# Attention as one table of fine steps, batched routing, and spaced place writes in a three-stage Trainium2 kernel

## The chip, the cores and the metric

One core of one Trainium2 chip runs the whole program. The metric is device time in microseconds for one execution. Engine names: PE is TensorE (matmuls and transposes), DVE is VectorE, ACT is ScalarE, POOL is GpSimd, SP is the engine that issues most DMAs.

## What is computed

Three layers in a row on float32 data, with B=2, H=8, S=768, D=48 and N=1536 tokens of width 384:

```python
# 1. gated linear attention, per head: a decaying, turning complex state
scale = min(|a|, 0.999) / (|a| + 1e-6);  a = (a_re + i a_im) * scale
S = a[t] * S + k[t] v[t]^T               # D x D per head, S complex
y[t] = q[t] @ Re(S)
# 2. a mixture of 8 experts, one per token, capacity 2N/E
e = argmax(x @ w_gate);  gate = softmax(x @ w_gate)[e]
out = gate * (relu(x @ w1[e]) @ w2[e])   # dropped beyond the capacity
# 3. RMS norm and a gated feed-forward layer
xn = x / sqrt(mean(x*x) + 1e-6) * rms_g
out = (silu(xn @ w_gate) * (xn @ w_val)) @ w_out
```

## The kernel before

**Order.** Every compute engine and SP is wrapped in `InOrder`, which chains the instructions of an engine in the order in which the program emits them. So the order of work on each engine is written by hand, and an engine whose next instruction waits holds back all that stands behind it.

**Attention** goes over 12 chunks of 128 tokens (six per sequence), with the gates of two chunks at a time in a group. For a group `squares`, `logs_1` to `logs_4` turn the gates into log decays and tangents (ACT with the table of Ln and Exp, DVE, and POOL for the sum of squares and one product), `sums` and `decays` make the running decay (PE, ACT) and send its last row to DRAM (`ends`), from which `ends_in` fetches it in another layout (`re`). `angles_1` to `angles_4` and `turns` make the running angle (ACT with the table of Arctan and Sin, PE, DVE). For a chunk `scaled` and `frame` form the turned keys and queries (DVE, `kqr`, `K`, `Q`), `flip` transposes them (PE, copied out by ACT as `KT`, `QT`), `scores` multiplies them (PE, tile `ap`) and masks them (DVE, `AT`), `end_decay` transposes `re` (PE, `rp`), `state_up` and `state` update the state (PE `up`, DVE `z`, POOL `st`), `outputs` forms the output (PE `yp`, copied out as `yT`) and `route_1` turns it back to token order and makes the routing logits (PE `xb`, DVE `lg_all`).

**Routing.** `choice` finds a token's expert by five small DVE instructions, `route_2` counts on PE (`rk`) which place a token has in its expert's list, `route_3` turns that into a slot by five more small DVE instructions, and `dispatch` writes the chunk's rows to the expert table `disp` in DRAM by an indirect DMA from POOL's queue. All of this goes chunk by chunk. `chunk(c, a, l)` writes out one chunk's steps with the angle steps of group `a` or the log steps of group `l` between them; a separate list writes out the start.

**The handover.** The first expert's rows are read back from `disp` (`xd_first`) and transposed; the rows of the last two chunks are added by a product with a 0/1 matrix `put`, made from the counts, so that no DMA stands between the last chunk and the first expert. The results `hi_first`, `lo_first` feed the first expert matmul `hp`.

**Experts.** 8 experts, each in 8 pieces of weights (four of w1 for `hp`, four of w2 for `op`). A weight is split into two parts, `hi` (ACT) and `lo` (DVE), so that three fast matmuls give full precision. `ahead(n)` runs at piece n: SP issues the load of piece n+8, and ACT and DVE split piece n+4. The weights of the third layer are loaded and converted in the same stage (`w_g`, `w_v`). `more_at` hangs extra work on single pieces: `meta_steps` at pieces 1 to 5 make the softmax weights and the places of the tokens in a list sorted by expert, `scatter(i)` for all 12 chunks at piece 6 writes place records of 12 bytes to DRAM (`packed`, three tables in turn, indirect DMAs on POOL's queue), `read_packed` at 7 reads them back, `join` at 30 merges them (DVE), and the gathers of the third layer's rows begin at 41.

**The third layer** (`gated`) is PE work from 307.75 us to the end.

Of the kernel before, what the change touches and what calls it, by code (L numbers as in the profile page):

```python
# [25 lines left out]
P = 128  # L26
# [6 lines left out]
W = 240  # L33
# [11 lines left out]
def tile_kernel(ctx: ExitStack, tc: tile.TileContext, q, k, v, a_re, a_im, gates, keys, vals, wg, w1, w2, cap, m_gate, m_val, m_out, rms_g, out, dbg=None):  # L45
# [276 lines left out]
    with ExitStack() as actx:  # L322
# [36 lines left out]

        def tiles(gi):  # L360
# [24 lines left out]
        def logs_3(gi, x=ALL):
            d = gd[gi]
            ea.activation(d["th"][:, x], d["th"][:, x], AF.Ln)
            ea.activation(d["th"][:, x], d["th"][:, x], AF.Exp, scale=-1.0)

        def logs_4(gi, x=ALL, e=None):  # L390
            d = gd[gi]
            (e or eg).tensor_tensor(d["th"][:, x], d["ai"][:, x], d["th"][:, x], ALU.mult)
            if 1 < gi < len(groups) - 2:
                load(gi + 2, ["g"])

        def sums(gi, js=range(GM)):
            for j in js:
                c = groups[gi][j]
                L = ps_cs.tile([P, H, D], F32, tag="cs", name=f"L_{c}")
                et.matmul(f2(L), tri, f2(gd[gi]["l2"][:, j]), start=True, stop=True)  # L400
                cd[c]["L"] = L

        def decays(gi, js=range(GM)):
            cs = [groups[gi][j] for j in js]
            for c in cs:
                R = cd[c]["R"] = ch.tile([P, 2, H, D], F32, tag="R", name=f"R_{c}", bufs=4)
                ea.activation(R[:, 0], cd[c]["L"], AF.Exp, scale=-0.5)
# [802 lines left out]
```

## Time and profile before

| | us |
|---|---|
| median of 3 runs | 542.95 (537.59 to 543.37) |
| the profiled execution, whole | 542.02 |
| its span, first to last instruction | 540.3 |
| attention: start to first `hp` | 0 to 161.03 |
| experts: first `hp` to first `gp` | 161.03 to 307.75 |
| third layer | 307.75 to the end |
| busy over the span: PE, DVE, ACT, POOL | 510.2, 328.7, 292.3, 100.9 |

A row of the timeline gives the start, the length, the engine, the instruction as out<-in, how many were merged (x), and in brackets the engine's idle time just before it with what ended it. An fp32 matmul stands as two records. "Granted clock" (PEclk) is the share of PE's full clock of 2.4 GHz; it has two levels, 1.00 and 0.50 (1.2 GHz).

### The profile page before, as it was taken

The numbers are of one execution on the slowest core, as the hardware profiler recorded it, in microseconds if no ns is written. First come the engines' busy times: TensorE is split into PE (matmuls) and PEld (weight loads), VectorE is DVE, ScalarE is ACT, GpSimd is POOL, SyncE is SP. The second block draws the span as 40 slices with busy tenths as digits, with TensorE's granted clock in tenths as the row PEclk, the third lists the DMA queues.
The fourth block names the chain that finished last, engine by engine and source line by source line (L and its number), as shares of the span: only waits on it lengthen the run. The fifth ranks groups of instructions, "written<-read, shape, count | busy, mean of one in ns | idle before, by whom it ended". The sixth has DMA issues, their size and how long they took to land. (4 is left out here: it accounts for less than half of the span.)

```text
span 540.3 us, 8701 instructions
## 1 busy us (share of the span) xinstructions
PE 510.2 (94%) x3297; PEld 452.0 (84%) x3298; DVE 328.7 (61%) x662; ACT 292.3 (54%) x492; POOL 100.9 (19%) x150
## 2 busy tenths in 40 slices
PE   6789998999888979999999999999999999999994
PEld 2467876778788979999999988899888899888894
DVE  4748798797746868899899887741144331333300
ACT  6868697795436647767788575732234321332200
POOL 5021442632710443000200030001400001000011
PEclk9979999999899989999999999999999999999998
DMA  8165704305315899999997263310221000000000
GB/s 310 29 244 196 258 24 166 129 0 176 103 59 204 210 236 270 353 292 322 319 347 246 87 179 110 93 30 30 84 64 32 28 15 30 16 1 0 2 31 33
DMA packets 30443, 72.40 MB, mean 134 GB/s; under 512 B 5853, under 2 KB 12537, under 8 KB 30393
## 3 DMA queue, kind: packets, MB, share of 16 engines
q1 hardware_dynamic: 25385, 61.66, 36.1%
q0 software_dynamic: 2832, 7.15, 3.9%
q10 hardware_dynamic: 2176, 2.95, 1.6%
q8 instruction: 28, 0.46, 0.4%
q14 instruction: 22, 0.18, 0.1%
HBM read 59.71 MB, written 12.04 MB: 133 GB/s over the span
## 5 line engine op out<-in xcount | busy, mean ns | idle before, releaser
L59 DVE TENSOR_TENSOR sg<-vp,sg 128x512 f32<-128x512 f32 x36 | 24.9, 691 | 77.3 <-PE vp L59 75.1
L59 DVE TENSOR_TENSOR lo<-raw,hi 128x768 fp32r<-128x768 f32 x60 | 57.0, 950 | 11.4 <-ACT hi L59 11.1
L59 ACT CAST hi<-raw 128x768 fp32r<-128x768 f32 x64 | 53.2, 836 | 15.1 <-DMA raw<-in_moe_w 5.7
L59 ACT CAST uh<-sg 128x512 fp32r<-128x512 f32 x36 | 22.4, 621 | 64.4 <-DVE sg L59 60.0
L59 POOL DMA_INDIRECT out<-ot,meta_in x12 | 11.7, 977 | 200.7 <-ACT ot L59 200.7
L59 PE MATMUL mop<-oh__3931,uh 128*128 128x384 f32 x144 | 48.9, 340 | 0.0
L59 PE MATMUL mop<-oh__3931,ul 128*128 128x384 f32 x144 | 48.4, 336 | 0.0
L59 PE MATMUL mop<-ol__3932,uh 128*128 128x384 f32 x144 | 48.4, 336 | 0.0
L59 PE MATMUL op<-hi,hh 128*128 128x384 f32 x128 | 45.8, 358 | 0.0
L59 PE MATMUL op<-hi,hl 128*128 128x384 f32 x128 | 43.9, 343 | 0.0
L59 PE MATMUL op<-lo,hh 128*128 128x384 f32 x128 | 43.9, 343 | 0.0
L59 ACT COPY ot<-mop 128x384 f32<-128x384 f32 x12 | 5.8, 480 | 53.4 <-PE mop L59 53.4
L59 DVE TENSOR_TENSOR ul<-sg,uh 128x512 fp32r<-128x512 f32 x36 | 24.8, 688 | 12.0 <-ACT uh L59 11.2
L59 POOL DMA_INDIRECT yt<-ybuf,meta_in x12 | 13.8, 1149 | 93.1 <-DMA raw<-in_moe_w 50.0
L59 PE MATMUL ap<-QT,KT 96*128 96x128 f32 x192 | 28.8, 297 | 2.3 <-DVE AT L59 1.6
L59 PE MATMUL gp<-mxh,gh 128*128 128x512 f32 x108 | 30.6, 391 | 0.0
L59 ACT ACTIVATE sg<-gp 128x512 f32<-128x512 f32 x36 | 21.5, 598 | 16.6 <-PE gp L59 15.7
L59 PE MATMUL gp<-mxh,gl 128*128 128x512 f32 x108 | 30.4, 389 | 0.0
L59 PE MATMUL gp<-mxl,gh 128*128 128x512 f32 x108 | 30.4, 389 | 0.0
L59 PE MATMUL vp<-mxh,vh 128*128 128x512 f32 x108 | 30.3, 389 | 0.0
L59 PE MATMUL vp<-mxl,vh 128*128 128x512 f32 x108 | 30.3, 389 | 0.0
L59 PE MATMUL vp<-mxh,vl 128*128 128x512 f32 x108 | 30.3, 389 | 0.0
(219 smaller groups left out, 1288.3 us busy)
## 6 DMA issues: line engine op xcount, KB each, us to landing
raw<-in_moe_w SPq DMA_DIRECT2D x64, 384.0 KB
w_g<-in_moe_w_gate SPq DMA_DIRECT2D x9, 512.0 KB
w_v<-in_moe_w_val SPq DMA_DIRECT2D x9, 512.0 KB
w_o<-in_moe_w_out SPq DMA_DIRECT2D x12, 384.0 KB
g<-in_gates SPq DMA_DIRECT2D x5, 768.0 KB
kq<-in_keys SPq DMA_DIRECT2D x5, 768.0 KB
v<-in_vals SPq DMA_DIRECT2D x12, 256.0 KB
disp<-zt SPq DMA_DIRECT2D x4, 768.0 KB
```

What stands on the lines that cost most here:

```text
L59: ins = getattr(self.eng, op)(*args, **kw)
```

## The change

The hand-written start, `chunk` and its loop are replaced by one table, `ORDER`, of 352 steps. A step is a name and a chunk or group (`u`, `w`: one chunk of a group); steps are emitted as they stand, so each engine gets its own part of the table in that order. A prime moves one instruction of the step to another engine: for `sq`, `q`, `z`, `p` from POOL to DVE, for `o`, `x`, `f1` (its Q half), `f0` the copy from ACT to DVE. The POOL keeps memsets and DMAs. The log and angle functions become single instructions (`la lb lc`, `m0 m1 m2`, `n0 n1`, `q`, `L R e`, `at a t ab sin`); `act` issues a table load whenever a step needs the other table, 16 in all where there were 12. `sc K Q f0 f1 s0 s1 ed up z o x` are `scaled`, the two `frame`s, the two halves of `flip` and `scores`, `end_decay`, `state_up`, `state`, `outputs`, `route_1`; `lg lk lv lz pl p` are loads, zeroing writes, loads and splits of the first weight pieces; `W` is warm-up matmuls. Routing of chunks 0 to 8 goes in three batches (`r1 r2 r3`); chunks 9 to 11 keep `choice` (`ch`) and `route_2` with `route_3` merged (`rt`). `put` is made by `mine` (`mi`) from the first expert's own logit and count, and the last chunk's choice and counting now stand behind the handover copies and ahead of the first `hp`.

In the expert stage the count steps of `meta_steps` come first, one step a piece; the scatters go one at a time at pieces 10, 12, ... 32, the read to 35 and the join to 39.

```diff
+        def act(need, out, x, func, **kw):
+
+            if table[0] != need:
+                ea.preload_act_table_set(need)
+                table[0] = need
+            ea.activation(out, x, func, **kw)
...
+            (e or eg).tensor_tensor(ns[:, :, :D], z, d["rT"][:, :, None].to_broadcast([2 * D, H, D]), ALU.mult)
...
+                (ea.copy if e is None else e.tensor_copy)(d["yT"][:, ps], yp[:, ps])
...
+            x_t = sm.tile([P, DM], F32, tag="x", name=f"x_{i}", bufs=5)
+            (ea.copy if e is None else e.tensor_copy)(x_t.rearrange("p (q d) -> p q d", q=4), xb[:, :, :2 * D])
...
+        def mine(i):
+
+            lg, mx = lg_all[:, i], mx_all[:, i]
+            ev.max(mx, lg)
+            own = sm.tile([P, 1], BF16, tag="own", name=f"own_{i}", bufs=2)
+            ev.tensor_scalar(own, lg[:, 0:1], mx[:, 0:1], None, ALU.is_ge)
+            r0 = ps_r.tile([P, 1], F32, tag="r", name=f"r0_{i}")
+            et.matmul(r0, ones_b, acc_oh[:, 0:1], start=True, stop=False)
+            et.matmul(r0, strict, own, start=False, stop=True)
+            own_f = sm.tile([P, 1], F32, tag="own_f", name=f"own_f_{i}", bufs=2)
+            ev.tensor_copy(own_f, own)
+            put = inp.tile([P, GM, 2, H, D], F32, tag="g", name=f"put_{i}").rearrange("p g r h d -> p (g r h d)")[:, :W]
+            ev.tensor_scalar(put, iota_w, r0, own_f, ALU.is_equal, ALU.mult)
+            cd[i]["put"] = put
...
+        def many_1(cs):
+            n, sl = len(cs), slice(cs[0], cs[-1] + 1)
+            ev.tensor_reduce(mx_all[:, sl, 0], lg_all[:, sl], AX.X, ALU.max)
+            eq = sm.tile([P, n, E], F32, tag="eq", name=f"eq_{cs[0]}", bufs=1)
+            ev.tensor_tensor(eq, lg_all[:, sl], mx_all[:, sl, 0:1].to_broadcast([P, n, E]), ALU.is_equal)
+            ev.tensor_tensor(eq, eq, rev8[:, None, :].to_broadcast([P, n, E]), ALU.mult)
+            fi = sm.tile([P, n, 1], F32, tag="fi", name=f"fi_{cs[0]}", bufs=1)
+            ev.tensor_reduce(fi[:, :, 0], eq, AX.X, ALU.max)
+            ev.tensor_tensor(oh_all[:, sl], eq, fi.to_broadcast([P, n, E]), ALU.is_equal)
+            end = sm.tile([P, n], F32, tag="ends", name=f"ends_{cs[0]}", bufs=1)
+            ev.tensor_scalar(end, fi[:, :, 0], -float(W), float((E + 1) * W), ALU.mult, ALU.add)
+            cd[cs[0]]["ends"] = end
+        def many_2(cs):
+            n, sl = len(cs), slice(cs[0], cs[-1] + 1)
+            rk = ps_r.tile([P, n, E], F32, tag="r", name=f"rks_{cs[0]}")
+            et.matmul(rk, ones_b, base_b[:, None, :].to_broadcast([P, n, E]), start=True, stop=False)
+            et.matmul(rk, ones_b, acc_oh[:, None, :].to_broadcast([P, n, E]), start=False, stop=False)
+            for j in range(n - 1):
+                et.matmul(rk[:, j + 1:], ones_b, oh_all[:, cs[j]][:, None, :].to_broadcast([P, n - 1 - j, E]), start=False, stop=False)
+            et.matmul(rk, strict, oh_all[:, sl], start=False, stop=True)
+            cd[cs[0]]["rks"] = rk
+        def many_3(cs):
+            n, sl = len(cs), slice(cs[0], cs[-1] + 1)
+            d = cd[cs[0]]
+            jk = sm.tile([P, n, E], F32, tag="eq", name=f"jks_{cs[0]}", bufs=1)
+            ev.tensor_tensor(jk, d["rks"], oh_all[:, sl], ALU.mult)
+            ev.tensor_reduce(slf_all[:, sl], jk, AX.X, ALU.add)
+            ev.tensor_tensor(d["ends"], slf_all[:, sl], d["ends"], ALU.is_ge)
+            ev.scalar_tensor_tensor(d["ends"], d["ends"], float(N * E), slf_all[:, sl], ALU.mult, ALU.add)
+            ev.tensor_scalar(slot_all[:, sl], d["ends"], spare, None, ALU.min)
+            so = sm.tile([P, E], F32, tag="so", name=f"so_{cs[0]}", bufs=1)
+            ev.tensor_reduce(so, oh_all[:, sl].rearrange("p c e -> p e c"), AX.X, ALU.add)
+            ev.tensor_tensor(acc_oh, acc_oh, so, ALU.add)
...
+        ORDER = """
+            sq.0u' sq.0w' la.0u lb.0u m1.0u lz.0 W.9 lc.0u m0.0u la.0w m2.0u n0.0u lb.0w m1.0w sq.1' n1.0u q.0u' L.0 n0.0w m0.0w lc.0w m2.0w la.1 n1.0w q.0w' lb.1 R.0 lc.1 m0.1 sc.0 at.0u W.27 at.0w lz.1 e.0 m1.1 a.0 t.0 ab.0u sin.0u Q.0 n0.1 K.0 W.6 m2.1 a.1 t.1 L.1 R.1 f0.0' n1.1 q.1' sc.1 lg.2 lg.3 ab.0w L.2 R.2 f1.0 s0.0
+            ed.0 at.1 up.0 z.0' s1.0 L.3 a.2 sc.2 sin.0w K.1 Q.1 e.1 R.3 o.0 t.2 e.2 sq.2' a.3 f0.1 x.0 la.2 t.3 f1.1 lk.2 s0.1 lz.4 ab.1 up.1
+            sin.1 ed.1 z.1' lb.2 s1.1 ed.2 Q.2 o.1 lc.2 K.2 f0.2 lv.3 lz.2 m1.2 n0.2 n1.2 f1.2 m0.2 e.3 m2.2 L.4 sc.3 q.2' L.5 R.4 R.5 e.4 lz.5 lz.3 x.1' s0.2
+            K.3 up.2 z.2' sc.4 at.2 sq.3' s1.2 Q.3 a.4 t.4 a.5 la.3 o.2' f0.3 t.5 ab.2 sin.2 ed.3 x.2 r1.0 f1.3
+            s0.3 K.4 lb.3 lc.3 up.3 z.3' lv.2 s1.3 Q.4 e.5 o.3 f0.4 m0.3 m1.3 r2.0 r3.0 m2.3 lg.4 x.3' d.0 s0.4 f1.4 sc.5 ed.4 Q.5 n0.3 lk.3 n1.3 L.6 L.7 R.6 R.7 K.5 up.4 q.3' lv.4 at.3 d.1
+            e.6 s1.4 o.4 a.6 a.7 z.4' t.6 sq.4' f0.5 x.4 t.7 f1.5 lg.5 e.7 ab.3 lk.4 sin.3
+            la.4 sc.6 s0.5 lb.4 ed.6 s1.5 o.5 lc.4 Q.6 K.6 f0.6 f1.6 m0.4 m1.4 n0.4 d.2 m2.4 L.8 R.8 sc.7 Q.7 x.5 r1.1 s0.6 L.9 n1.4 q.4'
+            lk.5 lv.5 K.7 up.6 R.9 z.6' r2.1 s1.6 at.4 a.8 r3.1 t.8 sq.5' a.9 o.6 sc.8 e.8 f0.7 e.9 x.6 t.9 d.3 d.4 ed.7
+            f1.7' ab.4 sin.4 la.5 s0.7 up.7 z.7' s1.7 pl.0 K.8 pl.1 Q.8 lb.5 m1.5 o.7 f0.8 lc.5 m0.5 m2.5 x.7' pl.2 f1.8 n0.5 n1.5 s0.8
+            sc.9 L.10 L.11 up.8 Q.9 R.10 R.11 e.10 q.5' at.5 s1.8 pl.3 K.9 pl.4 pl.5 pl.6 d.5 o.8 ed.8 pl.7 z.8' a.10 t.10 f0.9 a.11 sc.10 t.11 x.8' ab.5 r1.2 sin.5 s0.9 ed.9 Q.10
+            f1.9 K.10 up.9 r2.2 e.11 s1.9 r3.2 d.6 o.9 f0.10 z.9' x.9 sc.11 ed.10 f1.10 ch.9 s0.10 K.11 up.10
+            z.10' s1.10 Q.11 p.0' p.1' o.10 rt.9 f0.11 d.7 d.8 d.9 x.10 f1.11
+            mi.10 ch.10 s0.11 s1.11 p.2' p.3' o.11 rt.10 x.11' xd.0 d.10 fi.0 mi.11
+            pi.10 pi.11
+        """
+        for line in ORDER.strip().splitlines():
+            for step in line.split():
+                name, at = step.rstrip("'").split(".")
+                do[name](at, step.endswith("'"))
         for kk in range(KD):
+            ea.copy(first[0][:, kk], xps[kk])
+            ev.tensor_tensor(first[1][:, kk], xps[kk], first[0][:, kk], ALU.subtract)
+        choice(LAST)
+        route_2(LAST)
         dispatch(LAST)
...
-        more_at = {6: lambda: [scatter(i) for i in range(NT)], 7: read_packed}
-        for n in range(1, 6):
-            more_at[n] = lambda: list(islice(meta_todo, 2))
-        more_at[5] = partial(list, meta_todo)
-        more_at[30] = join
+        more_at = {10 + 2 * i: partial(scatter, i) for i in range(NT)}
+        for n in range(1, 9):
+            more_at[n] = partial(next, meta_todo, None)
+        more_at[9] = partial(list, meta_todo)
+        more_at[35] = read_packed
+        more_at[39] = join
```

## Rows read from the trace of the kernel before

**Rows 1.** Windows by stage: us; busy us by engine; granted clock; DMA share, GB/s
```profile
26.81:41.84 15.03, 13.25 (x83) 10.28 (x82) 6.85 (x12) 10.33 (x18) 2.77 (x3) 0.77 0.73 257
41.84:85.92 44.08, 42.29 (x391) 35.48 (x391) 38.53 (x95) 33.98 (x50) 18.37 (x15) 1.00 0.51 177
85.92:151.00 65.08, 59.38 (x549) 50.47 (x547) 51.61 (x138) 45.61 (x72) 28.16 (x23) 0.97 0.28 93
181.26:203.57 22.31, 19.36 (x128) 18.65 (x127) 16.22 (x26) 12.69 (x22) 8.15 (x8) 0.92 1.00 242
203.57:220.77 17.20, 17.20 (x127) 17.13 (x127) 15.36 (x26) 12.87 (x23) 4.55 (x4) 1.00 1.02 281
```

**Rows 2.** Timeline of PE: start us, us, instruction, [idle before]; chunk 0, chunk 4
```profile
30.96 0.21 PE L59 MATMUL rp<-ident,re 8*96 8x8 f32 x1 [1.78 <-DMA re<-ends]
35.02 2.82 PE L59 MATMUL TH<-th,tri_th 128*128 128x384 f32 x4
...
81.20 1.56 PE L59 MATMUL TH<-th,tri_th 128*128 128x384 f32 x4
```

**Rows 3.** Timeline of POOL, DVE and PE where POOL works beside DVE
```profile
52.17 1.83 POOL L59 TENSOR_TENSOR th<-g,th 128x768 f32<-128x768 f32 x1 [4.85 <-ACT th L59]
52.34 1.69 DVE L59 TENSOR_SCALAR oh_all<-iota,mf 128x8 bf16<-128x8 f32 x1
133.91 3.63 POOL L59 TENSOR_TENSOR lo<-raw,hi 128x768 fp32r<-128x768 f32 x2 [7.07 <-ACT hi L59]
135.79 2.58 DVE L59 TENSOR_TENSOR Q<-kqr,rot 128x768 f32<-128x768 f32 x1
138.42 0.64 PE L59 MATMUL Qp<-ident,Q 128*96 128x128 f32 x4 [1.76 <-DVE Q L59]
```

**Rows 4.** Groups by form: out<-in, shapes, count | busy us, mean ns | idle before
```profile
L59 ACT ACT_TABLE_LOAD x19 | 24.4, 1283 | 1.2 <-PEq L1181 0.8
L59 DVE TENSOR_TENSOR z<-up,st 96x384 f32<-96x384 f32 x8 | 4.4, 544 | 0.0
L59 DVE TENSOR_TENSOR th<-g,th 128x768 f32<-128x768 f32 x1 | 1.0, 958 | 0.7 <-ACT th L59 0.7
```

**Rows 5.** Timeline of DVE: one chunk's routing, and small operations on twelve chunks
```profile
123.16 0.14 DVE L59 TENSOR_SCALAR end<-mf 128x1 f32<-128x1 f32 x1
123.80 0.16 DVE L59 TENSOR_TENSOR acc_oh<-acc_oh,oh_all 128x8 bf16<-128x8 bf16 x1
130.09 0.17 DVE L59 MAX8 mx_all<-lg_all 128x8 f32<-128x8 f32 x1
130.76 0.23 DVE L59 TENSOR_SCALAR oh_all<-iota,mf 128x8 bf16<-128x8 f32 x1
168.84 0.24 DVE L59 TENSOR_REDUCE gw_all<-lg_all 128x12 f32<-128x96 f32 x1
```

**Rows 6.** First two experts: PE and ACT timeline; landing of the `packed` DMAs
```profile
169.74 0.38 PE L59 MATMUL cnt_n<-tri,cnt_sb 8*128 8x7 f32 x2 [1.36 <-DVE cnt_sb L59]
193.46 0.84 ACT L59 CAST hi<-raw 128x768 fp32r<-128x768 f32 x1 [4.07 <-DMA raw<-in_moe_w]
197.56 0.43 PE L59 MATMUL xp<-ident,xd 128*128 128x128 f32 x2 [2.44 <-DVE xl L59]
DMA to landing us min/median/max: 6.5/6.6/6.7
```

**Rows 7.** Handover: PE and DVE timeline; durations and landing of the `disp` DMAs
```profile
152.96 0.44 PE L59 MATMUL yp<-QT,st 96*64 96x128 f32 x4
161.03 0.45 PE L59 MATMUL hp<-hi_first,hi 128*128 128x240 f32 x1
161.80 0.41 DVE L59 TENSOR_TENSOR lo_first<-xp_first_u,hi_first 128x240 fp32r<-128x240 f32 x1
L59 POOL DMA_INDIRECT disp<-x,slot_all x12: 969/1024/1780, 54.2 to 163.6; - x12
DMA to landing us min/median/max: 2.5/2.9/3.3
```

More of the change, by code (lines that the diff above doesn't have):

```diff
@@ L392, in logs_4, with sums, decays @@
             (e or eg).tensor_tensor(d["th"][:, x], d["ai"][:, x], d["th"][:, x], ALU.mult)
[L393 to L407, printed above, removed]
-                ea.activation(R[:, 1], cd[c]["L"], AF.Exp, scale=0.5)
-                sp.dma_start(ends[c:c + 1], R[P - 1:P, 1])
+        def sums(c):
+            gi, j = group_of[c]
+            L = cd[c]["L"] = ps_cs.tile([P, H, D], F32, tag="cs", name=f"L_{c}")
+            et.matmul(f2(L), tri, f2(gd[gi]["l2"][:, j]), start=True, stop=True)
+        def decays(c):
+            R = cd[c]["R"] = ch.tile([P, 2, H, D], F32, tag="R", name=f"R_{c}", bufs=4)
+            act(LN, R[:, 0], cd[c]["L"], AF.Exp, scale=-0.5)
+            act(LN, R[:, 1], cd[c]["L"], AF.Exp, scale=0.5)
+            sp.dma_start(ends[c:c + 1], R[P - 1:P, 1])
         def ends_in(c):
@@ L551, in route_1 @@
             d["x"] = x_t
-            if not later:
-                choice(i)
         def choice(i):
@@ new lines, in tile_kernel, with first_in @@
+        first, xps = [], []
+        def first_in():
+            first.extend(wsp.tile([P, KD, W], F32R, tag=tg, name=f"{tg}_first", bufs=LS + 1) for tg in ("hi", "lo"))
+            xps.extend(p.tile([P, W], F32, tag=tg, name=f"xp_first_{tg}") for p, tg in ((ps_at, "at"), (ps_cs, "cs"), (ps_cs, "cs")))
+            for kk in range(KD):
+                for t, n in enumerate((P, REST)):
+                    et.matmul(xps[kk][:, t * P:t * P + n], cd[LAST]["xd"][:n, t, kk * P:(kk + 1) * P], ident[:n, :n], start=t == 0, stop=False)
@@ new lines, in put_in, with dispatch, xd_in @@
+        def put_in(c):
+            for kk in range(KD):
+                et.matmul(xps[kk], cd[c]["x"][:, kk * P:(kk + 1) * P], cd[c]["put"], start=False, stop=c == LAST)
+        def dispatch(i):
+            eg.indirect_dma_start(disp[:, :], bass.IndirectOffsetOnAxis(ap=slot_all[:, i:i + 1], axis=0), cd[i]["x"][:, :], None)
+        def xd_in():
+            xd = cd[LAST]["xd"] = inp.tile([P, GM, 2, H, D], F32, tag="kq", name="xd_first")[:, :, 0].rearrange("p g h d -> p g (h d)")
+            both_halves(xd, 0)
@@ L658, in tile_kernel @@
         ea.preload_act_table_set(LN)
+        table[0] = LN
         load(0, ["g"], True)
```

303 lines of the change are left out of this document (78 added, 225 removed).

## The prediction

> **What bounds the kernel now.** I read the windows by stage first. PE is full in the third expert, 17.20 of 17.20 us [rows 1], and the change touches neither the later experts' matmuls nor the third layer. So time can only come from attention, which ends at 161.03 us [rows 7], and from the first two experts, where PE has idle time. Then I read the idle brackets of PE's timeline there, since each names what was late.
>
> In the middle of attention (41.84 to 151.00, from the first scores of chunk 1 to those of chunk 11) PE is busy 42.29 + 59.38 = 101.7 of 109.2 us, DVE 90.1, ACT 79.6 [rows 1]. PE bounds it, with DVE close behind. Its idle 7.5 us, and the loss at the lower clock (0.97 granted over 65.08 us is 3.9 us at 1.2 GHz, so 1.95 us lost), make 9.4 us: no order of these steps can win more there, because PE's work stays the same apart from the routing counts.
>
> At the start PE waits 1.78 us for `re`, the row that goes through DRAM and back, and afterwards the clock is at 0.50: four `TH` records take 2.82 us at 35 us and 1.56 at 81 us [rows 2]. The window's mean clock of 0.77 over 15.03 us is 6.9 us at 1.2 GHz, 3.45 us lost [rows 1].
>
> In the second expert (22.31 us beside 17.20 for the third) ACT waits 4.07 us for a weight piece, PE then 2.44 us, and the clock falls (0.92: 1.8 us lost) [rows 1, 6]. The twelve place writes leave POOL in this stretch, each 6.6 us to landing [rows 6]; DMA is busy all the time and moves 242 GB/s where the next expert gets 281 [rows 1].
>
> **The start.** In the table `e.0` stands behind `R.0` and two zeroing writes. Before, `ends_in(0)` stood behind the decays of chunk 1 as well, which ACT makes only after two table loads. So `re` comes earlier by that wait, the 1.78 us go, and with them, probably, the low clock: 5.2 us at most. Against it stands one more table load ahead of chunk 1 (5 for 4), 1.28 us [rows 4] on the engine that the start leans on; that would leave 3.9. I take **-4.3**; the ends are -5.2 and 0 (another wait of the same length in its place).
>
> **The middle.** What DVE gets from POOL: 3 `sq` sums, 4 `q`, 4 `lo` at 0.95 to 0.96 us and 9 `z` products at 0.54 [rows 4] make 15.4 us; two copies from ACT (`o.2'`, `f1.7'`) about 0.6 each (as the 0.54 of the PSUM operand row) make 1.2. What it loses: routing costs a chunk 0.90 + 0.80 us (from the start of MAX8 to the end of `oh_all`, and from `end` to the end of `acc_oh` [rows 5]), 15.3 us for nine chunks; three batches of 13 small operations at no more than the 0.24 us of one on twelve chunks [rows 5] cost about 9.0; saved 6.3. And where POOL computes, DVE stands: an `oh_all` of 0.23 us took 1.69 while POOL's `th` ran (one of three such), a `Q` took 2.58 beside two `lo` on POOL, where its like take 0.96 [rows 3, 4]: 3 x 1.46 + 1.62 = 6.0 us saved. Net +4.3, so DVE has 94.4 us to do. ACT gets 11 table loads where it had 8, +3.8 us, and gives up 1.2: 82.2. Both stay under PE's 101.7, so nothing that moves becomes the bound by its sum; DVE would be at 90% of 104 us and can still be late for a single step.
>
> The one wait that I can name as gone is PE's 1.76 us for that `Q`, and the low clock behind it (1.95): 3.7 us. The rest of the 9.4 is small waits, mostly on a DVE queue with nine or ten full steps in a row; smaller routing and finer steps shorten those by an unknown part. I take **-5.0**; the ends are 0 and -9.4.
>
> The Trainium skill (ScalarE: Activation LUTs, section What ACT_TABLE_LOAD costs) counts a switch as a load of about 1283 ns and a drain of about 1380 ns. The load agrees with the 1283 ns here [rows 4]; by the page's whole price the four more switches would cost 10.6 us and not 5.1, an estimate.
>
> **The handover.** Before, `yp` of chunk 11 starts at 152.96 and the first `hp` at 161.03, 8.07 us later, and the last `lo_first` starts only at 161.80 [rows 7], so that the first products wait a little more for their operands, some 0.8 us. Now `put` needs fewer DVE operations (no index search), but the x copy of chunk 11 (about 0.5 us) stands on DVE ahead of it. And `choice(LAST)` with the three `rk` matmuls stands ahead of the first `hp` in PE's queue: after the last `lo_first` (0.41) come 0.7 us of choice (the 0.90 without MAX8) and the counting products, about 0.2. That is 1.7 us of PE idle for the 0.8 saved: +0.9. A pause like this may bring a half-clock stretch, which costs 1.7 to 1.9 where rows show one; three chances in ten, +0.5. I take **+1.4**; ends -0.5 and +4.
>
> Behind it: `d.6` to `d.9` write one table and go one at a time, 2.9 us each to landing [rows 7], 11.6 us, then `xd` is read, about 3 us more, before PE can transpose it. From the end of batch 3's routing to there PE has two whole chunks of work, about 17 us. So it is hidden, by two to three us.
>
> The Trainium skill (SBUF — State Buffer, section SBUF: two separate sides) says that certain DVE operations lock GpSimd out while it writes the descriptors of its own DMAs. By that, a fuller DVE would make these four writes later. The trace has one dispatch of 1780 ns beside a median of 1024 [rows 7]; four times that difference, 3.0 us, would just use up the cover, so the sum stays.
>
> **The experts.** The count's copy `cnt_sb` was late by 1.36 us for `cnt_n` one piece on [rows 6]. Now its copy stands first on DVE and two pieces (2 x 2.15 us, an eighth of 17.20) lie between: **-1.4** (ends 0 and -1.4). The scatters at every second piece, 4.3 us apart, are spread over 22 pieces, 47 us; the work of the DMA engines is the same, but pieces are loaded eight ahead, and a delay of a few us at a time is not passed on. Of the second expert's 22.31 - 17.20 = 5.1 us [rows 1] I take **-4.0** (ends 0 and -5.1). The last scatter goes at piece 32, and the join stands at 39, 15.1 us later; the scatter (1.0 and 6.6 us) and the last read, priced the same, need 15.2. So DVE may stand at the join for 0.1 to 2 us, with `lo`, `hl` and `xl` of the next pieces behind it and PE waiting for `xl`: **+0.5** (ends 0 and +2.2).
>
> **Sum.** -4.3 - 5.0 + 1.4 - 1.4 - 4.0 + 0.5 = -12.8, from the profiled execution's 542.02 to 529.2. The median of the runs is 0.9 above that execution; I say 529.5.
>
> **Rivals.**
> - *The middle gives nothing.* DVE at 90% keeps PE waiting as often as now. Speaks for it: nearly all small waits today are on DVE, and DVE has more to do. Against: its three 1.69 us blocks are gone. Time 529.2 + 5.0 = 534.2.
> - *The place writes still choke the weights.* The DMA is at 1.02 busy in the third expert too [rows 1], so there is little room for twelve slow writes wherever they stand; with a late join 529.2 + 4.0 + 1.7 = 534.9.
> - *The dispatch chain shows.* If the four writes take over 3.6 us each beside the loads `pl.5` to `pl.7`, PE waits for `xd`; at 5 us each 20 + 3 - 17 = 6, and 1.8 for the clock: 537.
> - *Slower: a wait at the head of a queue in every chunk of the middle.* The table gives chunks 1 and 2 five table loads (6.4 us) and the logs of two groups; each engine takes its steps strictly in order, and an early step that is not ready holds all behind it. Price: one wait like 1.78 us a chunk, ten of them, and the clock down after half, 5 x 1.8: 26.8 in place of the 9.4 now, +17.4 where I took -5.0: 529.2 + 22.4 = 551.6. It makes the kernel slower than before once the middle loses more than 9.4 + 7.8 = 17.2 us (the other terms give 7.8). Against it: no wait in the middle now is over 1.8 us, and ACT's sum is well below PE's.
> - *A table switch costs its drain too.* A drain would be idle ACT time at the load; ahead of all 19 loads the idle is 1.2 us [rows 4], so the trace speaks against it. Four more switches at twice the price would add 5.1: 534.3. This is the rule of the Trainium skill's ScalarE page above.
>
> **How the numbers follow.** Forecast 0.62, middle 0.13, place writes 0.09, dispatch 0.06, slower 0.07, drain 0.03. All gains at their ends make 5.2 + 9.4 + 0.5 + 1.4 + 5.1 = 21.6: 520.4. Upwards the range takes in the first three rivals and the fifth: 520 to 538, with about one in ten outside on the far side and some for two rivals at once. Runs of this kernel differ by about 1%, so I count 1% (5.4 us) as no change: below 537.5 counts as faster. Forecast and four rivals lie there, but two at once do not: faster 0.79, same 0.12, slower 0.09.
>
> **What would show it.** First scores of chunk 1 near 37.5 us and no low clock around 31 to 38; no DVE operation lengthened beside POOL; 104 us from there to the first scores of chunk 11; first `hp` near 153, after 1.5 to 2 us of idle PE behind `rk`; no ACT wait for `raw` above 2 us in expert 2, which lasts 17.2 to 18.5 us. The forecast is wrong if PE's idle in the middle is above 7 us, if `xp_first` waits for `xd`, or if a place write still stops `hi`.

## The result and the profile after

The changed kernel takes 534.21 us (median of 4 runs, 530.81 to 534.88) where the kernel before took 541.02 beside it (537.59 to 543.37): ratio 0.988, 95% interval 0.984 to 0.992. It is faster by 1.2%. Run again on another chip, beside the experiments, it gave 0.990 (0.988 to 0.993). The profiled execution is 534.88 us with a span of 533.2, 7.1 less than the 540.3 before, where the sum had 12.8. The 7.1 is made of larger terms of both signs.

The first view is the windows by stage, cut as in [rows 1] (us; busy us by engine with instructions; granted clock; DMA share, GB/s): the start, the middle (first scores of chunk 1 to those of chunk 11), the handover to the first `hp`, and experts 1 to 4.

```profile
25.37:35.94 10.57, 10.57 (x85) 8.52 (x84) 9.20 (x17) 10.04 (x15) 0.00 (x0) 1.00 0.54 171
35.94:137.63 101.69, 96.96 (x926) 83.32 (x924) 90.72 (x188) 80.99 (x121) 16.06 (x16) 1.00 0.39 131
137.63:155.65 18.02, 12.54 (x89) 11.16 (x88) 7.53 (x27) 4.13 (x9) 2.71 (x2) 0.81 0.32 102
155.65:174.25 18.60, 18.45 (x131) 17.94 (x132) 13.54 (x34) 11.24 (x18) 0.96 (x1) 1.00 0.67 225
174.25:191.41 17.16, 17.16 (x127) 17.09 (x127) 16.79 (x31) 12.94 (x22) 7.72 (x7) 1.00 1.01 286
191.41:208.83 17.42, 17.42 (x128) 17.06 (x128) 14.27 (x24) 12.03 (x23) 9.17 (x8) 1.00 0.99 263
208.83:231.25 22.42, 19.36 (x128) 18.66 (x128) 18.23 (x29) 13.68 (x24) 1.01 (x1) 0.92 0.97 286
```

Stage by stage, in us; the before column is from the same marks of the kernel before.

| stage | before | after | change | forecast |
|---|---|---|---|---|
| up to the first scores of chunk 1 | 41.84 | 35.94 | -5.9 | -4.3 |
| middle, to the first scores of chunk 11 | 109.16 | 101.69 | -7.5 | -5.0 |
| handover, to the first `hp` | 10.03 | 18.02 | +8.0 | +1.4 |
| expert 1 | 20.23 | 18.60 | -1.6 | -1.4 |
| experts 2 to 4 | 57.09 | 57.00 | -0.1 | -4.0 |
| experts 5 to 8 | 69.40 | 69.40 | 0.0 | +0.5 |
| third layer and end | 232.55 | 232.55 | 0.0 | 0.0 |

So attention won 13.4 us, and the handover gave 8.0 of them back. In experts 2 to 4 nothing was won: the second expert's stall of [rows 1, 6] is gone (22.31 to 17.16), and one of the same size stands in the fourth (17.58 to 22.42).

The handover first, on PE's, POOL's and SP's timelines (start us, us, instruction, [idle before and what ended it]).

```profile
142.75 0.61 PE L59 MATMUL xb<-pick,yT 128*128 128x104 f32 x4
147.61 1.20 PE L59 MATMUL xp_first_at<-ident,xd_first 128*128 128x128 f32 x4 [4.25 <-DMA xd_first<-disp]
...
155.65 0.38 PE L59 MATMUL hp<-hi_first,hi 128*128 128x240 f32 x1 [0.86 <-DVE lo_first L59]
```
```profile
127.06 0.97 POOL L59 DMA_INDIRECT disp<-x,slot_all  x1 [17.95 <-DVE z L59]
...
131.29 1.50 POOL L59 DMA_INDIRECT disp<-x,slot_all  x1 [2.90 <-DMA disp<-x,slot_all]
134.65 2.46 POOL L59 DMA_INDIRECT disp<-x,slot_all  x1 [1.86 <-DMA disp<-x,slot_all]
141.33 1.75 POOL L59 DMA_INDIRECT disp<-x,slot_all  x1 [4.22 <-DMA disp<-x,slot_all]
```

```profile
145.16 0.82 SPq L59 DMA_DIRECT2D xd_first<-disp  x2
```

PE has nothing left after `xb` and waits 4.25 us for `xd`. Behind the wait the clock is at half, 1.2 GHz: 0.81 over 18.02 us is 3.4 us lost. The four writes to `disp` leave at 127.06, 131.29, 134.65 and 141.33; SP issues the read of `xd` at 145.16. That is 18.1 us for the chain, and 2.45 more to `xp_first`.

The place writes, on POOL's timeline (the first, the last, the first read of the tables), and the fourth expert's stall, on ACT's and PE's:

```profile
175.30 1.68 POOL L59 DMA_INDIRECT packed<-meta,place  x1 [17.00 <-DVE meta L59]
...
202.75 1.13 POOL L59 DMA_INDIRECT packed<-meta,place  x1 [0.30 <-issue]
205.92 1.10 POOL L59 DMA_DIRECT2D meta<-packed  x1 [2.04 <-DMA packed<-meta,place]
```
```profile
216.85 0.57 ACT L59 ACTIVATE hh<-hp 128x480 fp32r<-128x480 f32 x1 [2.98 <-DMA raw<-in_moe_w]
```
```profile
225.19 0.43 PE L59 MATMUL xp<-ident,xd 128*128 128x128 f32 x2 [2.49 <-DVE xl L59]
```

In the program the twelve writes stand 4.3 us apart, over 47 us. On the chip they leave within 27.5 us, much as before (29.0, from 175.90 to 204.92). POOL has nothing else to do here: it sends each write as soon as `meta` is there and the earlier write to the same table has landed. A place in the program holds back an engine only if something ahead of it in that engine's own queue, or an operand, does.

### The profile page after: what moved, and what is told of

It is laid out like the page before. It is cut to its first block, busy times and chain, and to the rows that moved or that the text cites. A ratio compares the mean times of both kernels' runs of the same rounds, so it can differ in the third digit from the quotient of the medians.

```text
span 533.2 us, 8632 instructions
## 1 busy us (share of the span) xinstructions
PE 505.3 (95%) x3290; PEld 450.4 (84%) x3290; DVE 335.3 (63%) x631; ACT 294.6 (55%) x492; POOL 70.5 (13%) x128
## 5 line engine op out<-in xcount | busy, mean ns | idle before, releaser
L59 DVE TENSOR_TENSOR lo<-raw,hi 128x768 fp32r<-128x768 f32 x64 | 60.7, 951 | 6.2 <-ACT hi L59 5.5
L59 POOL DMA_INDIRECT out<-ot,meta_in x12 | 11.6, 969 | 200.8 <-ACT ot L59 200.8
L59 POOL DMA_INDIRECT disp<-x,slot_all x12 | 18.3, 1525 | 97.1 <-DVE acc_oh L59 53.7
```

The lines of the kernel that those rows point to most:

```text
L59: ins = getattr(self.eng, op)(*args, **kw)
```

## The experiments

The chips differ (the kernel before took 534.9 to 541.0 us on them), so ratios to the kernel before, measured beside each run, are compared, and stages from the profiles. Each kernel has one profile, the changed one two. "First hp" and the fourth expert are from the profiled executions; `h_` runs edit the handover, `p_` the place tables, `c_` the tables on top of both handover edits.

| run | what it is | us (before beside it) | ratio, 95% | first hp | expert 4 |
|---|---|---|---|---|---|
| after2 | changed kernel again | 530.37 (534.93) | 0.990 (0.988 to 0.993) | 154.59 | 21.41 |
| h_one | chunks 6 to 8 routed singly | 529.89 (536.62) | 0.990 (0.987 to 0.994) | 154.09 | 17.49 |
| h_loads | pieces 5 to 7 behind `xd` | 527.26 (536.62) | 0.984 (0.978 to 0.989) | 151.80 | 19.10 |
| h_both | both | 526.35 (536.62) | 0.981 (0.975 to 0.988) | 150.04 | 21.92 |
| p_burst | place writes together again | 532.13 (535.13) | 0.994 (0.992 to 0.997) | 156.81 | 17.18 |
| p_rows | tables read in 144-byte pieces | 528.79 (534.93) | 0.988 (0.986 to 0.991) | 154.92 | 17.18 |
| c_paced | h_both, place writes held back | 526.56 (535.13) | 0.984 (0.980 to 0.987) | 151.17 | 17.44 |
| c_rows | h_both and 144-byte pieces | 524.60 (535.13) | 0.981 (0.977 to 0.985) | 149.94 | 17.18 |
| c_prows | h_both, held back, 144-byte pieces | 524.57 (535.13) | 0.980 (0.976 to 0.984) | 150.84 | 17.44 |
| q_pool | elementwise steps back on GpSimd | 535.13 (534.93) | 1.001 (0.998 to 1.004) | 161.95 | 18.49 |
| s_late | read of chunk 0's `re` late | 539.04 (534.93) | 1.009 (1.005 to 1.012) | 164.95 | 17.78 |
| best | the edits that helped | 523.82 (538.62) | 0.973 (0.970 to 0.977) | 149.80 | 17.17 |

### The handover: h_one, h_loads, h_both

h_one puts the routing steps of single chunks in place of the third batch (pieces of the table's lines):

```diff
-            r1.2
-            r2.2
-            r3.2 d.6
-            rt.9 f0.11 d.7 d.8 d.9
+            ch.6
+            s0.7 rt.6 up.7 z.7' d.5 s1.7 d.6
+            ch.7
+            s1.8 rt.7 pl.3 K.9 pl.4 pl.5 pl.6 d.7
+            ch.8
+            rt.8 e.11 s1.9 d.8
+            rt.9 f0.11 d.9
```

> The changed kernel, but chunks 6, 7 and 8 are routed one at a time, each as soon as its x is there, and dispatched at once, where the changed kernel routes them as a batch at 126 us. Theory A (the four writes to one table start too late: 127.06, and take 18.1 us to the read of xd at 145.16): the writes of chunks 6 to 8 are gone by 135, only the one of chunk 9 is left, xd is read before 142, PE's 4.25 us wait at xp_first goes and with it the 6.83 us at half clock behind it. From the first scores of chunk 11 to the first hp it takes 10 to 11.5 us where it took 18.0; whole kernel 6 to 7 us faster than the changed one, about 527.5 to 528.5. The middle may lose up to 1 us, since DVE has some 2 us more to do. Theory B (it is the weight loads beside them that make these writes slow, whenever they leave): the write of chunk 9 alone still takes 5 us and more, xd comes at 145 or later, handover 15 us or more, less than 3 us gained.

Measured: handover 14.84 us, first `hp` at 154.09. The single writes were gone early, and still PE waited 2.26 us for `xd`. SP's queue shows why:

```profile
114.47 28.88 SPq L59 DMA_DIRECT2D raw<-in_moe_w  x5
143.45 0.64 SPq L59 DMA_DIRECT2D re<-ends  x2
144.29 0.82 SPq L59 DMA_DIRECT2D xd_first<-disp  x2
```

The read of `xd` stands behind the weight loads, the last of which waits for a buffer and is out only at 143.35. (In the changed kernel it is out at 141.73, so there the queue was ready and the chain set the time.) And the one write left, that of chunk 9, leaves POOL at 139.29 and takes 5.0 us to landing beside those loads, where the same write takes 2.6 in h_both. Both end at 144.3. Theory A alone would have given 10 to 11.5 us; it is a part of the cause. The whole kernel gained nothing by it: 0.990, as the changed kernel has, where 6 to 7 us were expected.

h_loads keeps the batch and moves three loads:

```diff
-            pl.3 K.9 pl.4 pl.5 pl.6 d.5 o.8 ed.8 pl.7 z.8'
+            pl.3 K.9 pl.4 d.5 o.8 ed.8 z.8'
-            xd.0 d.10
+            xd.0 pl.5 pl.6 pl.7 d.10
```

> The changed kernel with its batch of three kept, but the loads of weight pieces 5, 6 and 7 stand behind the read of xd in SP's queue, so that none of them runs beside the dispatch writes. Theory B (the loads slow the writes: 6.68 us from the start of chunk 8's write to that of chunk 9's, where the two before took 3.4 and 4.2): chunk 8's write takes 3.5 us, xd is there 3 us earlier or more, PE's wait at xp_first falls from 4.25 to under 1.5 us, handover 12 to 15 us for 18.0. Theory A (the chain starts too late, whatever runs beside it): the wait falls by less than 1.5 us, the half clock stays, handover 16.5 us or more. Either way the first expert may wait for pieces 5 to 7, by up to 2 us.

```profile
133.71 3.41 POOL L59 DMA_INDIRECT disp<-x,slot_all  x1 [1.87 <-DMA disp<-x,slot_all]
139.49 0.96 POOL L59 DMA_INDIRECT disp<-x,slot_all  x1 [2.37 <-ACT hi L59]
```
```profile
144.80 0.99 PE L59 MATMUL xp_first_at<-ident,xd_first 128*128 128x128 f32 x4 [1.43 <-DMA xd_first<-disp]
```

Measured: the chain from the first write to the issue of `xd` went from 18.1 to 15.4 us (127.07 to 142.45), the wait from 4.25 to 1.43, the handover to 14.16. So the loads cost the chain 2.7 us. But chunk 8's write, the slowest, is hardly shorter: 5.78 us to the next for 6.68. Its time went to something else too, since the issue on POOL alone takes 3.41 us where 0.96 is usual. DVE runs `Q` and two `lo` from 133.60 to 136.29 without a pause, and the issue ends 0.83 us after them. The first expert did not wait for the later loads (18.61 us).

> Both edits: chunks 6 to 8 routed and dispatched one at a time, and weight pieces 5 to 7 loaded behind the read of xd. If theory A is all of it, this is equal to the first of the two within 1 us (handover 10 to 11.5 us, about 528). If the loads matter by themselves too, it is 1 to 3 us better than the first. If the later loads cost the first expert a wait, it is up to 2 us worse than the first.

```profile
139.39:150.04 10.65, 9.43 (x88) 8.62 (x87) 7.54 (x27) 4.13 (x9) 1.92 (x2) 1.00 0.54 185
```

With both edits no wait for `xd` and no half clock are left, and the handover takes 10.65 us: 3.5 to 4.2 us less than with either alone. So both causes were there, and each was enough to make PE late. In the whole kernel h_both is 3.5 us under h_one and only 0.9 under h_loads (medians; the intervals overlap). What the handover loses goes in two parts, idle and clock: idle 5.48, 3.48, 2.67 and 1.22 us in the changed kernel, h_one, h_loads and h_both (window less PE's busy time), and 3.4, 1.6, 1.7 and 0 us by the granted clock (0.81, 0.89, 0.88, 1.00).

The price of single routing shows in the middle: 103.50 us for 101.69, with PE busy 98.16 for 96.96. Three chunks routed as a batch are thus worth 1.8 us. (In h_one, with the loads where they were, it is 103.36.) The counting products are the smaller part of it. A batch needs five where three single chunks need nine, but by their starts the batch's five hold PE for 0.13 us (123.19 to `ap` at 123.32), and the singles of h_both for 0.19, 0.15 and 0.11: about 0.3 us more in all. The rest fits DVE, which has 1.7 us more to do (92.43 for 90.72). One wait on it shows as idle time. Others stand under the modelled ends of matmuls and count as busy: the `yp` of 115.74 in h_both starts 0.48 us after the one before it, where 0.22 is usual, and 0.06 after DVE is done with its `AT`. First the changed kernel, then h_both:

```profile
123.19 0.18 PE L59 MATMUL rks<-base_b,ones_b 128*128 128x24 bf16 x1
```
```profile
103.28 1.13 PE L59 MATMUL ap<-QT,KT 96*128 96x128 f32 x8 [0.35 <-DVE junk L59]
```

### The place tables: p_burst, c_paced, c_rows, c_prows, after2, p_rows

```diff
-        more_at = {10 + 2 * i: partial(scatter, i) for i in range(NT)}
+        more_at = {10: lambda: [scatter(i) for i in range(NT)]}
...
-        more_at[35] = read_packed
-        more_at[39] = join
+        more_at[11] = read_packed
+        more_at[34] = join
```

> The changed kernel with one part undone: the twelve place writes are issued together at piece 10, the read of the tables at piece 11, the join at 34, as the kernel before had them (at 6, 7 and 30). Theory (the spacing in the program did nothing on the chip, because POOL has nothing else to wait for and sends the writes as soon as their operands and the table are free): the writes leave POOL at the same times as in the changed kernel within 2 us (175.30 to 202.75), experts 1 to 3 together take 57.0 us within 1.5, and the time is that of the changed kernel within 2 us. Rival (the spacing did help): experts 1 to 3 take 60 us or more, a stall of 4 to 5 us is back in the second expert and the one in the fourth stays.

The writes left at 176.47 to 202.37, as in the changed kernel: that the spacing does nothing held. But experts 2 to 4 took 51.53 us and not 57.0: there was no stall at all in this profile. The time, 0.994, is if anything worse than the changed kernel's 0.990 (the intervals overlap), and its ten runs spread from 529.07 to 534.78. So one profile does not tell what a part of the schedule is worth to the stall. That it comes and goes between runs of one kernel is likely but not shown: the four runs of h_both fall into two pairs, 528.17 (the profiled one, with its stall) and 528.50, and 524.50 and 524.54, nearly a stall apart. p_burst also loses 1.5 us in the middle, to a half clock that the changed kernel's profile does not have (last section).

c_paced holds the writes back in earnest, by an operand that DVE makes at the right piece:

```diff
         def scatter(i):
-            eg.indirect_dma_start(packed[i % 3][:, :], bass.IndirectOffsetOnAxis(ap=place[:, i:i + 1], axis=0), meta[:, i], None)
+            at = xs.tile([P, 1], I32, tag="at", name=f"at_{i}", bufs=3)
+            ev.tensor_copy(at, place[:, i:i + 1])
+            eg.indirect_dma_start(packed[i % 3][:, :], bass.IndirectOffsetOnAxis(ap=at[:, 0:1], axis=0), meta[:, i], None)
```

> The kernel with both handover edits, and with each place write held back by a small copy of its offsets on DVE, made at its own piece, so that POOL can't send it earlier: one every second piece, 4.3 us apart. Theory P (the burst of writes and the reads behind it take DMA from the weights; the fourth expert's 21.92 us where 17.2 is its work is their stall): spread over four experts each write costs the weights little at a time, every expert takes 17.2 to 17.6 us, total 4 to 5 us less than with the handover edits alone (about 521.5 to 522.5). Rival Q (the DMA engines have no room to spare: 0.92 to 0.95 busy in later experts without these writes; delays add up wherever the writes stand): the stall only moves on, to the fifth or sixth expert where the reads now stand, and the total is the same within 1.5 us.

The writes now leave from 176.72 to 224.11, and the fourth expert takes 17.44 us where h_both had 21.92. But the sixth takes 18.22 and the eighth 18.57 (17.20 and 17.83 in h_both), and the median is no better than h_both's (0.984 and 0.981). That is rival Q's sign, a stall that moves on, though what moved on is smaller in this profile than what went.

c_rows leaves the writes alone and changes the reads:

```diff
+            turn = xs.tile([P, 2, NT], I32, tag="turn", name="turn", bufs=1)
+            ev.tensor_scalar(turn[:, 0], place, P - 1, None, ALU.bitwise_and)
+            ev.tensor_scalar(turn[:, 1], place, 7, None, ALU.logical_shift_right)
+            ev.scalar_tensor_tensor(place, turn[:, 0], float(NT), turn[:, 1], ALU.mult, ALU.add)
...
-                eg.dma_start(meta_3[:, j], packed[j][0:N, :].rearrange("(t p) c -> p t c", p=P))
+                eg.dma_start(meta_3[:, j], packed[j][0:N, :].rearrange("(p t) c -> p t c", p=P))
```

> The kernel with both handover edits, and with the rows of the three place tables numbered so that each partition reads its twelve entries as one piece of 144 bytes instead of twelve of 12 bytes (384 pieces read instead of 4608); the writes stay as they are, three small operations are added on DVE. Theory R (the reads choke the weights in the fourth expert: they leave POOL at 197 to 202 and the late piece comes at 210.55): the fourth expert goes from 21.92 to under 18 us, total 4 us less. Theory P (it is the writes): landing of the reads gets shorter, but the fourth expert stays above 20 us.

> Both: place writes held to one every second piece, and the tables read in whole pieces. If the writes' burst is the only cause, equal to the held writes alone within 1 us; if only the reads matter, equal to the whole-piece reads alone; if the DMA engines are full anyway and both take room, better than either by 1 us or more, with every expert at 17.2 to 17.5 us and a total near 521.5.

Every expert from the second to the seventh takes 17.16 to 17.20 us in c_rows. Its runs lie within 2.0 us (523.68 to 525.67), where h_both's took 524.50 to 528.50. By the ratio it is no faster than h_both (0.981 both, on two chips), where theory R had 4 us. Holding the writes back as well adds nothing (c_prows, 0.980). The same edit alone on the changed kernel, with the changed kernel beside it on one chip:

> The changed kernel once more, on the chip of the runs beside it, so that single parts undone are compared with it on one chip. Expected: 0.985 to 0.992 of the kernel before; stages as in the first profile (first scores of chunk 1 at 35.9, of chunk 11 at 137.6, first hp at 155.6 us), except the fourth expert, which other runs showed at anything from 17.2 to 22.4 us.

> The changed kernel with nothing changed but the numbering of the place tables' rows, so that the three reads take 384 pieces of 144 bytes and not 4608 of 12. Theory R (the reads of the tables take the DMA from the weights; in the changed kernel the moved bytes fall to 25 to 120 GB/s while they run): the fourth expert falls from 22.4 to under 17.6 us, 4.5 to 5 us less than the changed kernel where that has its stall. Theory P (the writes): it stays above 20 us, same time within 1.5 us. Chance (the stall comes and goes with small shifts, and neither is its cause): the fourth expert is at any value, and the spread of the runs' times is as wide as that of the changed kernel (4 us and more).

The fourth expert goes from 21.41 to 17.18 us. The DMA view of both, 195 to 215 us in slices of half a microsecond, shows the place; after2 first, then p_rows (busy tenths of the DMA engines; GB/s moved).

```profile
DMA  9999899976896699951965379899999999999999
GB/s 356 379 412 374 154 374 396 215 99 209 344 330 225 250 346 389 339 116 10 61 16 16 100 258 316 348 380 315 222 207 179 138 184 267 280 237 298 335 339 335
```
```profile
DMA  9999979789786998859686959989999999999999
GB/s 369 373 403 347 235 188 357 249 182 221 274 231 258 381 266 269 340 198 190 172 320 174 195 205 352 275 315 363 347 387 307 292 307 319 416 365 401 350 391 392
```

While the three reads of 1536 pieces of 12 bytes run (issued from 201.43 to 205.35), the bytes moved fall to 10 to 116 GB/s for 3 us; with 128 pieces of 144 bytes each they never fall below 172. One read of 18 KB took 8.3 us to land in the changed kernel (median of the three), and 3.1 in the last kernel below.

By the medians the edit is worth 1.6 us (0.990 to 0.988, the intervals overlap): the profiled run of the changed kernel on that chip was its slowest of six, 532.48, and the others took 529.40 to 530.69. So the reads empty the weight stream where the fourth expert stalls, and none of the four profiles with 144-byte pieces has the stall (17.17 to 17.44 us). The reads of 12 bytes are not enough for it by themselves: p_burst and h_one read the same way and took 17.18 and 17.49. Why the second expert's stall of the kernel before went away stays open. The writes begin 19.7 us after the first `hp` now, and began 14.9 after it before; no run moved that alone.

### GpSimd's elementwise steps: q_pool

```diff
-            sq.3' sq.4' sq.5'
-            q.2' q.3' q.4' q.5'
-            z.1' z.2' z.3' z.4' z.6' z.7' z.8' z.9' z.10'
-            p.0' p.1' p.2' p.3'
+            sq.3 sq.4 sq.5
+            q.2 q.3 q.4 q.5
+            z.1 z.2 z.3 z.4 z.6 z.7 z.8 z.9 z.10
+            p.0 p.1 p.2 p.3
```

> The changed kernel with the elementwise steps of the middle back on GpSimd as the kernel before had them: 3 sums of squares, 4 products q, 9 products z, 4 lo. Theory M1 (while POOL computes, DVE operations beside it are drawn out, and POOL takes 1.8 us where DVE takes 0.95): from the first scores of chunk 1 to those of chunk 11 it takes 2 to 6 us more than the changed kernel's 101.7, and single DVE operations of 1.5 us and more show again beside POOL's. Theory M2 (DVE was nearly full, at 90 of 101.7 us, so taking 15.4 us of work off it shortens its waits): 0.5 to 2 us less than 101.7. Another loss is possible by order: z stands behind dispatch writes in POOL's queue, which wait 2 to 4 us for the write before.

```profile
36.00:141.62 105.62, 97.99 (x925) 83.86 (x924) 87.98 (x170) 81.58 (x121) 37.41 (x34) 0.99 0.37 128
```
```profile
70.62 2.00 POOL L59 TENSOR_TENSOR th<-g,th 128x768 f32<-128x768 f32 x1 [1.67 <-ACT th L59]
...
134.07 3.57 POOL L59 TENSOR_TENSOR lo<-raw,hi 128x768 fp32r<-128x768 f32 x2
```
```profile
70.84 2.60 DVE L59 TENSOR_TENSOR K<-kqr,rot 128x768 f32<-128x768 f32 x1
...
134.07 4.39 DVE L59 TENSOR_TENSOR Q<-kqr,rot 128x768 f32<-128x768 f32 x1
```

The middle takes 105.62 us, 3.9 more, and the whole gain of the change is lost (1.001; 4.8 us more than the changed kernel on that chip). DVE gave up some 13.5 us of work in this window (two of the `lo` lie behind it) and is busy only 2.7 us less (87.98 for 90.72): six of its operations, one of them in the handover, stand drawn out beside POOL's, `K` at 2.60 us and `Q` at 4.39 for 0.95. M1 is right, M2 is wrong. What part is DVE standing beside POOL and what part POOL's longer steps (2.00 us for `th`, where DVE takes 0.95) was not separated; about 1 of the 3.9 us is the lower clock (0.99). The handover loses 2.3 us more, with the dispatches behind `lo` in POOL's queue. The Trainium skill (SBUF — State Buffer, section Who interferes with whom) says that a DVE instruction with two SBUF inputs contends with a GpSimd one that reads SBUF, and the later one waits; both `K` and `Q` are such, and the trace agrees.

### The start: s_late

```diff
-            lz.1 e.0 m1.1
+            lz.1 m1.1
-            L.2 R.2 f1.0
+            L.2 R.2 e.0 f1.0
```

> The changed kernel with one step moved: the read of chunk 0's decay ends from DRAM (e.0) stands behind the decays of chunk 2 on SP's queue, near where the kernel before had it in time (25.5 us; 16.0 in the changed kernel). Theory S1 (the wait for re and the half clock behind it are the start's loss): PE waits 2 to 5 us for re at about 26.5, the clock falls to half after it, and the first scores of chunk 1 move from 35.94 to 39.5 to 42; total 3.5 to 6 us more. Theory S2 (the start gains by the finer steps and the order, re is only one wait among others): no half clock, first scores of chunk 1 before 38.5, total under 2.5 us more.

```profile
32.22 0.22 PE L59 MATMUL rp<-ident,re 8*96 8x8 f32 x1 [5.49 <-DMA re<-ends]
32.36 2.80 PE L59 MATMUL up<-v,K 128*96 128x48 f32 x16
```

`re` is issued at 26.83 and used at 32.22, 5.4 us later, as in the kernel before (25.51 to 30.96). PE waits 5.49 us, the clock falls (0.74 over 19.83 us, 5.2 us lost), and the window of the start goes from 10.57 to 19.83 us. Total 8.7 us more than the changed kernel. S1 is right in kind, and too small in size: it had the first scores of chunk 1 at 39.5 to 42 and 3.5 to 6 us in all, and they came at 45.50. The wait is longer than the 1.78 us of [rows 2] for three reasons: the read comes 1.3 us later than there, chunk 0's scores are 1.1 us earlier, and `up`, which filled 1.5 us of the gap there, stands behind `rp` in the table.

### The edits together: best

Handover edits, but chunks 6 and 7 as a batch of two and chunk 8 alone, and the tables in 144-byte pieces as in c_rows (pieces of the table's lines, and the new steps):

```diff
+            t1=of_pair(many_1), t2=of_pair(many_2), t3=of_pair(many_3),
...
+            t1.2
+            s1.8 t2.2 t3.2 pl.3 K.9 pl.4 d.6 d.7
+            ch.8
+            rt.8 e.11 s1.9 d.8
+            rt.9 f0.11 d.9
+            xd.0 pl.5 pl.6 pl.7 d.10
```

> Meant to beat both kernels: the changed kernel with chunks 6 and 7 routed as a batch of two and chunk 8 alone, each dispatched at once; weight pieces 5 to 7 loaded behind the read of xd; place tables read in pieces of 144 bytes. Expected from the single edits: no wait of PE for xd and no half clock in the handover (10.7 us from the first scores of chunk 11 to the first hp), no stall in the fourth expert (17.2 us), and in the middle about half of the 1.8 us that routing three chunks one at a time cost: first scores of chunk 11 near 138.5, first hp near 149.2, span near 521. If the batch of two dispatches chunk 7 too late, PE waits for xd and the first hp is at 151 or later.

```profile
35.95:139.17 103.22, 97.65 (x928) 83.43 (x926) 91.74 (x199) 81.02 (x121) 11.56 (x16) 1.00 0.37 125
139.17:149.80 10.63, 9.41 (x88) 8.62 (x87) 7.53 (x27) 4.13 (x9) 1.92 (x2) 1.00 0.54 184
```

0.973 of the kernel before (0.970 to 0.977), faster than both; its runs lie within 1 us. The first `hp`, expected near 149.2, came at 149.80: the batch of two brought only 0.3 us of the 0.9 expected in the middle (103.22 for 103.50).

## Why the prediction was right, and where not

The kernel got faster, by about half of what the sum had, and its time lies in the range (529.5 forecast, 534.2 measured, range 520 to 538). That it lies there owes something to luck: two gains were larger than their terms by 4.1 us together, and two other terms failed by 10.5. Of its own signs of being wrong one came outright, `xp_first` waiting for `xd`.

- **The start, -4.3, measured -5.9.** The mechanism is shown by s_late. The window from the first scores of chunk 0 on gave 15.03 to 10.57, that is -4.5, close to the term. The rest, 1.4, is that the scores of chunk 0 themselves came at 25.37 and not 26.81; the term left out what finer steps do ahead of its window, so its end of -5.2 was no bound.
- **The middle, -5.0, measured -7.5.** DVE did not become the bound: 90.72 of 101.69 us, for 94.4 forecast. The reason for the bound of -9.4, that PE's work stays the same, did not hold. Idle time fell by 2.8 us (7.5 to 4.7), PE's busy time by 4.7, and of that the clock explains 1.95 at most. Of the other 2.8 about 1.0 are the counting products, which the prediction named and gave no price: by their starts nine single ones of 0.15 us before (145.71 to `yp` at 145.86 is one), three batches of 0.13 now. The rest is open; waits that count as busy, as in h_both, would fit. The term was mis-sized in what it took for "an unknown part": 1.3 us behind the 3.7 of the one named wait, where 3.8 came. The move off GpSimd, priced at 6.0 us of DVE, is worth 3.9 us of the stage (q_pool).
- **The handover, +1.4, measured +8.0.** This step failed. The part that was priced, `rk` ahead of the first `hp`, came out at about 1 us idle (0.86 and 0.15). The part that was called hidden "by two to three us" was not: the chain takes 18.1 us to the issue of `xd` for the 11.6 forecast, against a cover of 16.3 (127.06 to `xb`'s end at 143.36) for 17. The price of 2.9 us for a write [rows 7] is the middle of two writes only, 3.3 and 2.5 us: for the other ten the trace of the kernel before tells no landing. A slow one was in it. The write of 119.84, with the first weight loads beside it, held the next back to 125.83, 6.0 us:

```profile
125.83 1.02 POOL L59 DMA_INDIRECT disp<-x,slot_all  x1 [2.35 <-DMA disp<-x,slot_all]
```
```profile
122.11 22.96 SPq L59 DMA_DIRECT2D raw<-in_moe_w  x8
```

In the chain the four land in 4.0, 3.1, 5.9 and 3.8 us, beside weight loads (2.7 us by h_loads) and beside DVE operations that hold up the issues. The 3.0 us that the prediction worked out from the long dispatch of 1780 ns [rows 7] (three others took 1620 to 1660) is nearly what the issues took in the end: 0.97 + 1.50 + 2.46 + 1.75 = 6.7 for four times 0.96, so 2.8. It was found to use up the cover, and then left out of the sum and of the rival's chance.
- **The rival "the dispatch chain shows"**, at 0.06, came true: its place, its mark (PE waits for `xd`) and its size, 6 us of wait and 1.8 for the clock where 4.3 and 3.4 were measured. Its total of 537 is 2.1 above the profiled 534.9, the sum of errors of both signs.
- **The count, -1.4, measured -1.6** on expert 1, with `cnt_n` not waiting. Right.
- **The place writes, -4.0, measured -0.1.** "Spread over 22 pieces" failed: the spacing is not in the queue. And the cost was put on the writes alone; the reads behind them empty the stream more deeply (p_rows). The rival "the place writes still choke the weights" meets the total, 534.9, by luck: its stall came, in another expert, but not its late join, and the handover and the larger gains are not in it.
- **The join, +0.5, measured 0.** The writes were done early, so nothing waited.
- **The other rivals fell.** The middle gave something; no wait of PE in it was above 1.12 us. The table switch has no drain of its own: 23 loads where there were 19, and still 1.2 us of idle ahead of them all, where the Trainium skill (ScalarE: Activation LUTs, section What ACT_TABLE_LOAD costs) has 1380 ns for each.

```profile
L59 ACT ACT_TABLE_LOAD x23 | 29.5, 1283 | 1.2 <-PEq L1142 0.8
```

Slips in the working that change nothing above: 39 small operations at 0.24 us make 9.4 and not 9.0; 529.2 and 0.9 make 530.1 and not 529.5; and the 6.6 us [rows 6] taken for each of the twelve place writes are the middle of one write (6.5) and one read (6.7). In the changed kernel the writes took 5.9 to 8.1 to landing.

## What to carry to other kernels

A step that is called hidden needs its price from rows taken under the load it will meet. Here 14.6 us were put under a cover of 17, and the case that it shows got 0.06. To space out work on an engine that is otherwise idle, tie it to an operand that another engine makes at the right time: a place in the program does not hold it back. When a stall seems to be due to many small transfers, change the size of the pieces before their time.

## What the runs showed of the hardware

An indirect DMA's issue on POOL is drawn out beside DVE operations with two operands in SBUF. In the changed kernel one took 4.31 us where the usual is 0.96, and ended 0.85 us after the last of four such operations. The three long ones of the handover (1.50, 2.46 and 1.75 us) ended 0.83 to 0.84 us after theirs. No run moves such an operation alone; this is read from the times.

```profile
104.59 4.31 POOL L59 DMA_INDIRECT disp<-x,slot_all  x1 [2.40 <-DMA disp<-x,slot_all]
```
```profile
104.50 0.94 DVE L59 TENSOR_TENSOR K<-kqr,rot 128x768 f32<-128x768 f32 x1
105.36 0.95 DVE L59 TENSOR_TENSOR Q<-kqr,rot 128x768 f32<-128x768 f32 x1
106.23 0.95 DVE L59 SCALAR_TENSOR_TENSOR th<-g,sq 128x768 f32<-128x768 f32 x1
107.10 0.95 DVE L59 SCALAR_TENSOR_TENSOR sq<-sq 128x768 f32<-128x768 f32 x1
```

And the same pause of PE does not always bring the half clock. In the changed kernel and in p_burst PE waits 1.12 us for `KT` at the same place, 86.17 and 86.16 us; over the same window, 84.70 to 94.00, the clock is 1.00 in the one and 0.82 in the other, the latter first here:

```profile
84.70:94.00 9.30, 8.18 (x59) 6.90 (x57) 7.56 (x15) 7.81 (x14) 0.00 (x0) 0.82 0.25 94
```
```profile
84.70:94.00 9.30, 7.48 (x62) 6.20 (x60) 8.97 (x18) 9.02 (x16) 0.00 (x0) 1.00 0.32 106
```

That is 1.7 us between two runs with the same schedule up to there. After the waits for `xd_first` and `re` (1.43 us in h_loads, 2.26 in h_one, 4.25 in the changed kernel, 5.49 in s_late) the clock fell each time, but in h_loads a later one of 1.71 us left it at 1.00:

```profile
219.36 0.43 PE L59 MATMUL xp<-ident,xd 128*128 128x128 f32 x2 [1.71 <-DVE xl L59]
```
```profile
219.36:226.36 7.00, 7.00 (x49) 7.00 (x50) 6.96 (x12) 4.70 (x8) 0.00 (x0) 1.00 0.85 281
```

So the length of a wait alone does not tell. best, where PE waits no longer than 1.12 us from 6 us on to the end of the experts, is also among those whose runs agree most closely (523.73 to 524.69).
